# Splitting the transfers of the attention phase into pieces of 0.13 to 0.26 MB

## The chip, the core and the metric

The kernel runs on one core of a Trainium2 chip. Time is the device time of one execution in microseconds (us); the runs of the kernel before are summed up as a median of three. The engines are PE (TensorE), ACT (ScalarE), DVE (VectorE), POOL (GpSimd) and SP (SyncE), which here does nothing but issue transfers (DMAs) between the chip's memory (DRAM) and the core's own memory.

## What is computed

A chunked attention whose output is the input of a mixture of 8 experts with a dense, Sinkhorn-balanced routing. Cut to what matters:

```python
# q, k, v: (4, 8, 768, 64); mem_k, mem_v: (4, 8, 8, 64)
for c in range(24):                       # chunks of 32 queries, in each of 4 batches
    ctx = slice(max(0, 32*c - 16), min(768, 32*c + 32 + 8))
    k_full = concat(mem_k, k[:, :, ctx]); v_full = concat(mem_v, v[:, :, ctx])
    a = softmax(q[:, :, 32*c:32*c+32] @ k_full.T / 8)
    out[:, :, 32*c:32*c+32] = a @ v_full
x = out as (3072 tokens, 512)
P = exp(x @ w_gate - max);  8 times: P /= row sums; P /= column sums; P *= 3072 / 8
y = sum over e of P[:, e] * (relu(x @ w1[e]) @ w2[e])      # w1: 512x1024, w2: 1024x512
```

## The kernel before

The tokens are worked through in 24 attention blocks of 128 tokens (`n` = 0 to 23), which make 6 units of 512 tokens (`u` = 0 to 5). Attention is fp32 on PE and is woven into the products of the first expert (`e` = 0) for the early units: the products of unit 0 are plain, those of later units and experts take seven products in place of eight (operands with sums and differences, each kept as two fp16 halves). Then follow experts 1 to 7 over all 6 units.

A small scheduler (`Plan`) sets the order in which each engine gets its instructions. Every piece of work is a task with an engine, a cost, a priority (its due time) and the tasks it depends on; `Plan.run` walks through a modelled clock for each engine and takes the ready task of least priority. A transfer is a task of SP: it is charged 0.5 us of SP's clock for each DMA it issues (`cost * ISSUE`) and its `dma` figure on a modelled common DMA clock. So the number of DMAs of a task is an input of the scheduler, and the order on PE, ACT, DVE and POOL can change with it. What it decides is fixed when the program is built; on the chip each engine runs its list in order and waits by semaphores.

The transfers that matter here, all from SP:

- `load_block(n)`: q and k of a block into one of two buffers each. Before, q is one DMA of 0.26 MB, and k one (two where a batch begins). The buffer of block n is that of block n - 2, so its load waits until PE has turned that block (`tq_n`, `tk_n`: four transposes on PE of q and of k).
- `load_values(n)`: v of a block, 8 to 10 DMAs of at most 57 KB, and small copies of the memory rows inside the core (`v_pair<-v_pair`, `x_room<-x_room`). `load_extra(u)`: the few k rows past the end of each block (`kx`).
- `load(e, fp, which, ...)`: a quarter of an expert's weights, 0.52 MB, w1 as two DMAs and w2 as one. It serves the first look at a weight for its maximum (`ahead="m"`, tiles `w1fm`, `w2fm`) and the load for cutting it into operands (`w1f`, `w2f`; in `weights`, for expert 0 a second time).
- `build(u, at)` makes a unit's operands `x_u`; its `keep` stores them in DRAM as `xkeep_u`, one DMA of 1.84 MB with 14336 bytes a partition. There are six, and later experts load them back.
- For units 4 and 5 the tokens themselves (`xg_g`) are stored (`gkeep_g`) and loaded back (`xs_g`), 0.52 MB each.
- `akeep_T`: the outputs of 128 tokens, 0.26 MB, stored and later loaded again.

SP issues in one order. The framework gives SP's DMAs eight semaphores in turn, and each DMA waits for the one eight places ahead of it.

On PE the names are: `tq_n`, `tk_n`, `sp_n`, `ta_n`, `xp_n`, `xt_n` for the steps of an attention block (transposes of q and k, scores, transposes of the weights, weights times v, transposes of the result); `pp` and `yp` for the plain products of unit 0; `px`, `py`, `pz` and `yx`, `yy`, `yz` for the products of the others. Where the scheduler expects PE to have no work for more than 0.4 us, `Plan.pad` fills in products on a constant (`warm`).

Of the kernel before, what the change touches and what calls it, by code (L numbers as in the profile page):

```python
# [233 lines left out]
def tile_chunked_attn_sinkhorn_moe(  # L234
# [27 lines left out]
    nc = tc.nc  # L262
    P = 128
    B, H, S, D = q.shape
# [3 lines left out]
    CH, LC, RC = 32, 16, 8  # L268
    QB = P
# [7 lines left out]
    HP = H // 2  # L277
    KT = DM // P
# [7 lines left out]
    DH = DM // 2  # L286
    BU = UT // QB
# [46 lines left out]
    xkeep = [dram.tile([P, 2 * 7 * 2 * GT], F16, name=f"xkeep_{u}") for u in range(NU)]  # L334
    gkeep = [dram.tile([P, KT * GT], F32, name=f"gkeep_{g}") for g in range(2 * NU)]
# [3 lines left out]
    add = plan.add  # L339
# [193 lines left out]
    wo = {}  # L533
    known = {}

    def load(e, fp, which, prio, ahead="", eng="SP", after=()):
        shape = [P, 2, KT, P] if which == 1 else [P, 2, DM]
        place = "stage", stage
        if (e, which) == (0, 2) and ahead == "" and fp < 2:

            place = ("ws", "ss")[fp], comb
        st = buf(*place, shape, F32, f"w{which}f{ahead}_{e}_{fp}")

        queue = nc.scalar if eng == "ACT" else nc.sync

        def go():
            if which == 1:
                for fh in range(2):
                    queue.dma_start(st.t[:, fh], w1v[e, fp, :, :, fh])
            else:  # L550
                queue.dma_start(st.t, w2v[e, fp])

        return st, add(eng, 2 if which == 1 else 1, go, after, prio, [st], dma=2.1)

    def most(e, fp, which, st, deps, prio):
        def go():
# [160 lines left out]
        wo[0, fp, 2] = (first2[fp], [done])  # L717

    def weights(e, fp, which, prio):
        st, ld = load(e, fp, which, prio - 25)  # L720
        cut(e, fp, which, st, ld, prio)


# [36 lines left out]
    def rows(src, b, t, m):  # L760
        return src[b, :, t : t + m].rearrange("h t d -> t h d")
# [70 lines left out]
    def load_block(n):  # L832

        b, blk = divmod(n, NB)
        t0 = blk * QB
        at = needed(n) - 25.0 if n >= BU else BLOCKS[n]
        qt = buf("q", att, [P, H, D], F32, f"q_{n}")
        kt = buf("k", att, [P, H, D], F32, f"k_{n}")

        def go_k():  # L840
            if blk == 0:
                nc.sync.dma_start(kt.t[0:LC], rows(k, b, 0, LC))
                nc.sync.dma_start(kt.t[LC:P], rows(k, b, 0, P - LC))
            else:
                nc.sync.dma_start(kt.t, rows(k, b, t0 - LC, P))

        lq = add(
            "SP", 1, lambda: nc.sync.dma_start(qt.t, rows(q, b, t0, QB)), (), at, [qt], dma=1.55
        )
        lk = add("SP", 2 if blk == 0 else 1, go_k, (), at + 0.1, [kt], dma=1.55)  # L850
        state[n] = (qt, kt, lq, lk)

    vs = {}
# [258 lines left out]
    def values(n, s, made):  # L1112

        vt, lv = vs[n]
        at = needed(n) - 4.0
        aT = buf("at", att, [P, HP, QB], F32, f"at_{n}")
        tp = bank("att", [P, HP, QB], f"ta_{n}")
        xp = bank("early" if n == 1 else "two", [P, 2, 512], f"xp_{n}")
        tx = bank("att", [P, HP, QB], f"xt_{n}")
        g, o = divmod(n * QB, GT)  # L1120
        if g not in halves:
            halves[g] = (buf("g", att, [P, KT, GT], F32, f"xg_{g}"), [])
        gt = halves[g][0]

        def go_t():
            for i in range(HP):
                nc.tensor.transpose(  # L1127
                    tp.t[:, i], s.t[:, 2 * i : 2 * i + 2].rearrange("p h d -> p (h d)"), ident
                )

        def go():
            for i in range(HP):
                for c in range(CB):
                    cs = slice(c * CH, (c + 1) * CH)
                    for par in range(2):
                        r = slice(par * D, (par + 1) * D)
                        nc.tensor.matmul(  # L1137
                            xp.t[cs, par, i * DV : (i + 1) * DV],
                            aT.t[r, i, cs],
                            vt.t[r, c, i],  # L1140
                            start=True,
                            stop=True,
                        )

        t = add("PE", 0.5, go_t, [made], at, [s, aT], takes=tp)
        t = add("ACT", 0.6, lambda: nc.scalar.copy(aT.t, tp.t), [t], at, [aT], frees=tp)
        t = add("PE", 0.9, go, [t] + lv, at + 2, [vt, aT], takes=xp, many=n > 1)
        after_v.append(t)
        xq = buf("at", att, [P, HP, 2, D], F32, f"xq_{n}")
        rec = buf("sm", att, [P, H], F32, f"rec_{n}")  # L1150

        def share():
            x = xp.t[:, :, 0 : HP * DV].rearrange("p a (i d) -> p a i d", d=DV)
            r = rec.t.rearrange("p (a i) -> p a i", a=2)
            nc.vector.tensor_scalar_add(r, x[:, :, :, D], 1e-9)
            nc.vector.reciprocal(rec.t, rec.t)
            nc.vector.tensor_tensor(
                xq.t.rearrange("p i a d -> p a i d"),
                x[:, :, :, 0:D],
                r[:, :, :, None].broadcast_to([P, 2, HP, D]),  # L1160
                op=ALU.mult,
            )

        t = add("DVE", 1.1, share, [t], at + 2, [xq, rec], frees=xp)
        if n == 1:

            def hand_over(t=t):
                pstack.close()
                late["ps"] = ctx.enter_context(tc.tile_pool(name="pl", bufs=1, space=PSUM))
                del plan.free["early"]  # L1170
                for b in range(2):
                    heappush(plan.free["main"], (t.end + 0.2, b))

            add("-", 0.0, hand_over, [t], -2000.0, takes=Bank("early", lambda b: None))

        def go_x():
            for i in range(HP):
                nc.tensor.transpose(tx.t[:, i], xq.t[:, i].rearrange("p a d -> p (a d)"), ident)  # L1178

        t = add("PE", 0.5, go_x, [t], at + 2, [xq, gt], takes=tx)  # L1180
        t = add(
            "ACT",
            0.6,
            lambda: nc.scalar.copy(gt.t[:, :, o : o + QB], tx.t),
            [t],
            at + 2,
            [gt],
            frees=tx,
        )
        halves[g][1].append(t)  # L1190
        if n % (GT // QB) == GT // QB - 1 and g > 1:

            col = BU + g - 2

            def most():
                nc.vector.tensor_reduce(
                    vmax[:, col : col + 1],
                    gt.t.rearrange("p k n -> p (k n)"),
                    axis=AX.X,
                    op=ALU.max,  # L1200
                    apply_absolute_value=True,
                )

            at = needed(n) - 1.0
            vfound.append(add("DVE", 1.21, most, halves[g][1], at, [gt]))
            if g % 2:
                scale_x(n // BU, vmax[:, col - 1 : col + 1], vfound[col - 1 : col + 1], at)
        if g >= 2 * KEEP:
            if n % (GT // QB) == GT // QB - 1:
                gkept[g] = add(  # L1210
                    "SP",
                    1,
                    lambda: nc.sync.dma_start(gkeep[g], gt.t.rearrange("p k n -> p (k n)")),
                    halves[g][1],
                    needed(n) + 4.0,
                    [gt],
                    dma=2.1,
                )
        elif n % BU == BU - 1:
            build(n // BU, needed(n))  # L1220
        if n % BU == BU - 1:
            logits(n // BU, needed(n) + 6.0)
# [3 lines left out]
    def rebuild(u, at):  # L1226

        for g in (2 * u, 2 * u + 1):
            st = buf("stage", stage, [P, KT, GT], F32, f"xs_{g}")
            ld = add(  # L1230
                "SP",
                1,
                lambda st=st, g=g: nc.sync.dma_start(
                    st.t.rearrange("p k n -> p (k n)"), gkeep[g]
                ),
                [gkept[g]],
                at - 12.0,
                [st],
                dma=2.1,
            )  # L1240
            halves[g] = (st, [ld])
        build(u, at)


    def build(u, at):
# [4 lines left out]
        ready = c1 + c2 + [sxs[u]]  # L1250

        def keep(at, done):
            xkept[u] = add(
                "SP",
                1,
                lambda: nc.sync.dma_start(xkeep[u], x.t.rearrange("p a o k n -> p (a o k n)")),
                done,
                at + 10.0,
                [x],
                dma=7.0,  # L1260
            )
# [917 lines left out]
    for fp, s in enumerate(fetch_first(1, START)):  # L2179
# [9 lines left out]
        dma=0.3,  # L2189
# [3 lines left out]
    for n, (e, u) in enumerate(units):  # L2193
# [80 lines left out]
        if n >= NU and n % NU < NU - 2:  # L2274
# [16 lines left out]
                        dma=7.0,  # L2291
# [36 lines left out]
```

## Time and profile before

| what | value |
|---|---|
| median of 3 runs | 1921.87 us (1920.07 to 1922.44) |
| the profiled execution | 1919.81 us |
| its span, first to last instruction | 1917.9 us |
| granted TensorE clock | 1.000 |
| transfers | 254.82 MB in 246791 packets, 133 GB/s over the span |

The span is divided by engine and by stretch of time; a stretch of 40 or 50 us shows PE's busy time in it, the share of time for which the 16 DMA engines were busy, and the rate. The times of SP in the timeline are those of the issuing instructions: the shortest of most kinds take 0.32 to 0.39 us, and the time until the data has landed is not in them.

### The profile page before, as it was taken

The page shows a single profiled execution, that of the slowest core. Times are in us where ns is not written, and L with a number is a line of the kernel's source. Part 1 is how long each engine was busy: PE and PEld are TensorE (multiplying, and loading weights), DVE is VectorE, ACT ScalarE, POOL GpSimd, SP SyncE. Part 2 cuts the span into 40 slices and gives each one's busy share as a digit, 9 for nine tenths or more (in the row PEclk, how much of TensorE's full clock was granted, in tenths as well). Part 3 has the DMA queues.
Part 4 walks back from the last instruction along what each step waited for, and adds up shares of the span by engine and source line. Part 5 has one row for each costly group of instructions (what it writes and reads, how often), then busy time and mean ns, then how long its engine had stood idle before and what let it go on. Part 6 is the DMA issues. An engine that isn't in the chain of part 4 may idle for free.

```text
span 1917.9 us, 47295 instructions
## 1 busy us (share of the span) xinstructions
PE 1903.2 (99%) x19616; PEld 1641.0 (86%) x19616; DVE 1436.4 (75%) x2396; ACT 1033.6 (54%) x2019; POOL 524.4 (27%) x549
## 2 busy tenths in 40 slices
PE   9999999999999999999999999999999999999999
PEld 7777676688888888888888888888888888888888
DVE  6776569778679866898668875898678885786565
ACT  4765565556456545646445554655555554564453
POOL 1220001544224221432124231342124232332112
PEclk9999999999999999999999999999999999999999
DMA  8678753453235342265214533245313732322321
GB/s 198 174 194 209 171 172 116 129 204 125 83 110 172 127 148 85 78 197 185 92 63 149 197 105 127 78 160 176 138 45 105 242 122 94 100 83 84 127 83 67
DMA packets 246791, 254.82 MB, mean 133 GB/s; under 512 B 113264, under 2 KB 180272, under 8 KB 242224
## 3 DMA queue, kind: packets, MB, share of 16 engines
q1 hardware_dynamic: 244452, 251.21, 41.2%
q8 instruction: 153, 2.51, 0.6%
q10 hardware_dynamic: 2124, 0.59, 0.2%
q14 instruction: 62, 0.51, 0.1%
HBM read 187.84 MB, written 63.44 MB: 131 GB/s over the span
## 4 chain that ended last, share of the span: by engine, by line
PE 96%; DMA 2%; DVE 1%; ACT 0%; issue 0%; SPq 0%; ACTq 0%; DVEq 0%
PE px L1598 26%; PE yx L1598 23%; PE pz L1598 13%; PE yz L1598 11%; PE py L1598 6%; PE yp L2126 6%; PE yy L1598 6%; DMA q<-in_q_dram 1%; PE xp L1137 1%; PE sp L1069 1%; PE pp L2045 1%; PE tq L1006 1%; PE tk L1010 0%; PE ta L1127 0%; PE xt L1178 0%; DVE w L521 0%
## 5 line engine op out<-in xcount | busy, mean ns | idle before, releaser
L1598 PEld LDWEIGHTS <-w 128*128 128x128 f16 x7896 | 771.4, 98 | 91.9 <-issue 0.6
L1598 PEld LDWEIGHTS <-h 128*128 128x128 f16 x7056 | 690.4, 98 | 81.4 <-issue 1.5
L1598 PE MATMUL px<-x,w 128*128 128x256 f16 x4512 | 549.1, 273 | 0.0
L1931 POOL TENSOR_TENSOR acc<-acc,y 128x256 f32<-128x256 f32 x252 | 267.5, 1068 | 862.1 <-ACT y L1906 842.7
L1598 PE MATMUL yx<-w,h 128*128 128x256 f16 x4032 | 467.5, 273 | 1.3 <-DVE acc L1941 1.3
L1657 ACT ACTIVATE q<-px 128x256 f32<-128x256 f32 x376 | 142.8, 381 | 294.2 <-PE px L1598 289.5
L1598 PE MATMUL pz<-x,w 128*128 128x256 f16 x2256 | 278.2, 273 | 0.0
L1598 PE MATMUL yz<-w,h 128*128 128x256 f16 x2016 | 233.8, 273 | 0.0
L1826 DVE TENSOR_TENSOR h<-ss,h 128x1024 f16<-128x1024 f32 x160 | 215.0, 1346 | 4.0 <-ACT h L1802 3.5
L1777 ACT ACTIVATE h<-c 128x768 f16<-128x768 f32 x168 | 140.8, 838 | 106.4 <-DVE c L1667 106.4
L1802 ACT CAST h<-ss 128x1024 f16<-128x1024 f32 x168 | 174.1, 1039 | 20.4 <-DVE ss L1766 19.6
L1766 DVE SCALAR_TENSOR_TENSOR ss<-c,ss 128x256 f32<-128x256 f32 x336 | 168.3, 501 | 8.2
L1810 DVE SCALAR_TENSOR_TENSOR h<-c,h 128x768 f16<-128x768 f32 x168 | 165.3, 984 | 9.2 <-ACT h L1777 9.1
L1667 DVE SCALAR_TENSOR_TENSOR c<-px,q 128x256 f32<-128x256 f32 x188 | 78.0, 422 | 103.2 <-PE px L1598 94.9
L1906 ACT ACTIVATE y<-yx,pscale 128x256 f32<-128x256 f32 x168 | 79.4, 473 | 114.8 <-PE yx L1598 110.6
L1598 PE MATMUL py<-x,w 128*128 128x256 f16 x1128 | 139.2, 273 | 0.0
L2126 PE MATMUL yp<-w,h 128*128 128x512 f16 x576 | 132.0, 379 | 0.0
L1667 DVE SCALAR_TENSOR_TENSOR c<-py,q 128x256 f32<-128x256 f32 x188 | 78.5, 422 | 60.2 <-PE py L1598 56.7
L1766 DVE SCALAR_TENSOR_TENSOR ss<-c,h 128x512 f32<-128x512 f32 x168 | 120.8, 719 | 3.1 <-ACT h L1754 3.0
L1598 PE MATMUL yy<-w,h 128*128 128x256 f16 x1008 | 116.9, 273 | 0.0
L2126 PEld LDWEIGHTS <-h 128*128 128x128 f16 x576 | 56.0, 98 | 57.9
L513 ACT ACTIVATE w<-ws,sw 128x1024 f16<-128x1024 f32 (+1 forms) x64 | 69.3, 1089 | 65.5 <-POOL ws L602 65.5
(158 smaller groups left out, 1773.0 us busy)
## 6 DMA issues: line engine op xcount, KB each, us to landing
x<-xkeep SPq DMA_DIRECT2D x28, 1792.0 KB
akeep<-acc SPq DMA_DIRECT2D x168, 256.0 KB
acc<-akeep SPq DMA_DIRECT2D x168, 256.0 KB
w1f<-in_moe_w_dram SPq DMA_DIRECT2D x72, 256.0 KB
w2f<-in_moe_w_dram SPq DMA_DIRECT2D x32, 512.0 KB
w1fm<-in_moe_w_dram SPq DMA_DIRECT2D x56, 256.0 KB
w2fm<-in_moe_w_dram SPq DMA_DIRECT2D x28, 512.0 KB
xkeep<-x SPq DMA_DIRECT2D x6, 1792.0 KB
```

Source lines behind the costliest of these rows:

```text
L513: lambda: nc.scalar.activation(dst(0), src(), AF.Copy, scale=s),
L1598: nc.tensor.matmul(dst.t, a, b, start=(not more and n == 0), stop=(n == end), skip_group_check=more,)
L1657: lambda: nc.scalar.activation(t.t, src.t, AF.Copy, scale=DOWN),
L1667: lambda: nc.vector.scalar_tensor_tensor(c.t[:, o], src.t, DOWN, q.t, op0=ALU.mult, op1=ALU.add),
L1766: lambda: nc.vector.scalar_tensor_tensor(dst(), src(), 0.0, other(), op0=ALU.max, op1=op),
L1777: lambda: nc.scalar.activation(h.t[:, 0, 0:3], c.t, AF.Relu),
L1802: lambda: nc.scalar.copy(h.t[:, 0, 3:7], ss.t),
L1810: lambda: nc.vector.scalar_tensor_tensor(h.t[:, 1, 0:3].rearrange("p a n -> p (a n)"), c.t.rearrange("p a n -> p (a n)"), 0.0, h.t[:, 0, 0 ...
L1826: lambda: spare.tensor_tensor(h.t[:, 1, 3:7], ss.t, h.t[:, 0, 3:7], op=ALU.subtract),
L1906: (lambda: nc.scalar.activation(t.t, src.t, AF.Copy, scale=f))
L1931: lambda: nc.gpsimd.tensor_tensor(acc.t[:, cols], acc.t[:, cols], q.t, op=ALU.add),
L2126: nc.tensor.matmul(py.t, hf.t[:, hl, where[fh], o : o + P], room(fp, WIDE * wl + DM * fh, WIDE * wl + DM * (fh + 1)), start=(fp == 0 and i ...
```

## The change

The diff in full, but for some lines of context:

```diff
+    def each(to, of):
+        for i in range(KT):
+            nc.sync.dma_start(to[:, i], of[:, i])
+
-    def load(e, fp, which, prio, ahead="", eng="SP", after=()):
+    def load(e, fp, which, prio, ahead="", eng="SP", after=(), again=False):
...
+        parts = KT if (e, ahead) == (1, "m") or (e == 0 and again) else 1
+
         def go():
-            if which == 1:
+            if parts > 1:
+                for i in range(KT):
+                    j, k = i // 2, slice(i % 2 * 2, i % 2 * 2 + 2)
+                    if which == 1:
+                        queue.dma_start(st.t[:, j, k], w1v[e, fp, :, k, j])
+                    else:
+                        d = slice(i % 2 * DH, (i % 2 + 1) * DH)
+                        queue.dma_start(st.t[:, j, d], w2v[e, fp, :, j, d])
+            elif which == 1:
                 for fh in range(2):
                     queue.dma_start(st.t[:, fh], w1v[e, fp, :, :, fh])
             else:
                 queue.dma_start(st.t, w2v[e, fp])
 
-        return st, add(eng, 2 if which == 1 else 1, go, after, prio, [st], dma=2.1)
+        return st, add(eng, max(parts, 2 if which == 1 else 1), go, after, prio, [st], dma=2.1)
...
     def weights(e, fp, which, prio):
-        st, ld = load(e, fp, which, prio - 25)
+        st, ld = load(e, fp, which, prio - 25, again=True)
...
                 nc.sync.dma_start(kt.t[LC:P], rows(k, b, 0, P - LC))
+            elif n < BU:
+                nc.sync.dma_start(kt.t, rows(k, b, t0 - LC, P))
             else:
-                nc.sync.dma_start(kt.t, rows(k, b, t0 - LC, P))
+                halved(kt.t, rows(k, b, t0 - LC, P))
+
+        def halved(to, of):
+            for h in (slice(0, HP), slice(HP, H)):
+                nc.sync.dma_start(to[:, h], of[:, h])
+
+        def go_q():
+            if n < BU:
+                nc.sync.dma_start(qt.t, rows(q, b, t0, QB))
+            else:
+                halved(qt.t, rows(q, b, t0, QB))
 
         lq = add(
-            "SP", 1, lambda: nc.sync.dma_start(qt.t, rows(q, b, t0, QB)), (), at, [qt], dma=1.55
-        )
-        lk = add("SP", 2 if blk == 0 else 1, go_k, (), at + 0.1, [kt], dma=1.55)
+            "SP", 1 if n < BU else 2, go_q, (), at, [qt], dma=1.55
+        )
+        lk = add("SP", 1 if n < BU and blk else 2, go_k, (), at + 0.1, [kt], dma=1.55)
...
                 gkept[g] = add(
                     "SP",
-                    1,
-                    lambda: nc.sync.dma_start(gkeep[g], gt.t.rearrange("p k n -> p (k n)")),
+                    KT,
+                    lambda: each(gkeep[g].rearrange("p (k n) -> p k n", k=KT), gt.t),
...
             ld = add(
                 "SP",
-                1,
-                lambda st=st, g=g: nc.sync.dma_start(
-                    st.t.rearrange("p k n -> p (k n)"), gkeep[g]
-                ),
+                KT,
+                lambda st=st, g=g: each(st.t, gkeep[g].rearrange("p (k n) -> p k n", k=KT)),
...
         def keep(at, done):
+            def go():
+                to = xkeep[u].rearrange("p (a o k) -> p a o k", a=2, o=7)
+                for i in range(7):
+                    nc.sync.dma_start(to[:, :, i], x.t[:, :, i].rearrange("p a k n -> p a (k n)"))
+
             xkept[u] = add(
                 "SP",
-                1,
-                lambda: nc.sync.dma_start(xkeep[u], x.t.rearrange("p a o k n -> p (a o k n)")),
+                7,
+                go,
```

Here `KT` = 4, `BU` = 4, `H` = 8, `HP` = 4, `DH` = 256. So q and k come in halves of four heads from block 4 on (k not where a batch begins, which was two DMAs already); the second load of expert 0's w1 and the first look at expert 1's weights come in four; the stores and loads of the kept tokens in four; each `xkeep` in seven, one for each operand block, in pieces of 1024 bytes. Nothing else of the computation changes. SP issues 125 DMAs more, all between about 36 us and 320 us of the profiled execution; before and behind that the orders of all engines are the same.

In that stretch the scheduler also arranges the work anew. The first place is SP's list around the store of unit 0's operands and the loads of block 8 (`q_8`, `k_8`). Before:

```order
L549 DMA w1f_0_0_1408<-in_moe_w1_dram 128x4x128 x2
L2150 DMA akeep_0_134<-acc_0_0_1398 128x512
L549 DMA w1f_0_1_1423<-in_moe_w1_dram 128x4x128 x2
L1256 DMA xkeep_0_116<-x_0_626 128x7168
L848 DMA q_8_1463<-in_q_dram 128x8x64
L845 DMA k_8_1564<-in_k_dram 128x8x64
L790 DMA kx_2_1589<-in_k_dram 32x8x64 x3
L787 DMA kx_2_1589<-in_k_dram 16x8x64
```

and now:

```order
L2179 DMA akeep_0_134<-acc_0_0_1403 128x512
L1280 DMA xkeep_0_116<-x_0_626 256x1x512 x7
L557 DMA w1f_0_0_1516<-in_moe_w1_dram 128x2x128 x4
L557 DMA w1f_0_1_1574<-in_moe_w1_dram 128x2x128 x4
L865 DMA q_8_1604<-in_q_dram 128x4x64 x2
L865 DMA k_8_1622<-in_k_dram 128x4x64 x2
L804 DMA kx_2_1669<-in_k_dram 32x8x64 x3
L801 DMA kx_2_1669<-in_k_dram 16x8x64
```

The same bytes stand ahead of `q_8`, with the store now ahead of both weights; `q_8` was SP's 118th DMA and its halves are the 135th and 136th.

The second place follows on it, up to the load of block 9. Before:

```order
L788 DMA kx_2_1589<-in_k_dram 16x8x64
L549 DMA w1f_0_2_1670<-in_moe_w1_dram 128x4x128 x2
L890 DMA v_pair_159<-in_mem_v_dram 8x4x64 x2
L921 DMA v_pair_159<-in_v_dram 56x4x64 x8
L549 DMA w1f_0_3_1789<-in_moe_w1_dram 128x4x128 x2
L2150 DMA akeep_1_135<-acc_0_1_1461 128x512
L848 DMA q_9_1810<-in_q_dram 128x8x64
L845 DMA k_9_1846<-in_k_dram 128x8x64
L898 DMA v_pair_159<-v_pair_159 8x3x260 x2
```

and now:

```order
L802 DMA kx_2_1669<-in_k_dram 16x8x64
L557 DMA w1f_0_2_1720<-in_moe_w1_dram 128x2x128 x4
L916 DMA v_pair_159<-in_mem_v_dram 8x4x64 x2
L947 DMA v_pair_159<-in_v_dram 56x4x64 x8
L557 DMA w1f_0_3_1860<-in_moe_w1_dram 128x2x128 x4
L924 DMA v_pair_159<-v_pair_159 8x3x260 x2
L2179 DMA akeep_1_135<-acc_0_1_1461 128x512
L865 DMA q_9_1905<-in_q_dram 128x4x64 x2
```

Between the kx row of 16 that ends the first place (L787, now L801) and `q_9` stood 16 DMAs, and now 22: four more by the weights' quarters, and the two copies inside `v_pair`, which came behind block 9's q and k before.

The third place is PE's list at the same point: the four transposes of q of block 8 (`tq_8`). Rows of one product that repeat are left out. Before:

```order
L1137 MATMUL xp_6_1723<-x_room_163,at_6_1648 32x65 x32
L1006 MATMUL tq_8_1757<-ident_98,q_8_1463 128x128 x4
L2045 LDWEIGHTS w1_0_3_708
L2045 MATMUL pp_0_1_3_0_1711<-x_0_626,w1_0_3_708 128x256
...
L1010 MATMUL tk_8_1776<-ident_98,k_8_1564 128x128 x4
L1178 MATMUL xt_6_1783<-ident_98,xq_6_1765 128x128 x4
L1127 MATMUL ta_7_1792<-ident_98,s_7_1673 128x128 x4
```

and now:

```order
L1163 MATMUL xp_6_1725<-x_room_163,at_6_1658 32x65 x32
L2074 LDWEIGHTS w1_0_3_707
L2074 MATMUL pp_0_1_3_0_1708<-x_0_626,w1_0_3_707 128x256
...
L2155 LDWEIGHTS h_0_0_806
L2155 MATMUL yp_2_1771<-w2_0_0_1101,h_0_0_806 128x512
...
L1204 MATMUL xt_6_1791<-ident_98,xq_6_1768 128x128 x4
L1153 MATMUL ta_7_1797<-ident_98,s_7_1680 128x128 x4
L1032 MATMUL tq_8_1803<-ident_98,q_8_1604 128x128 x4
```

Six `pp` products, six `yp` products and eight transposes now stand between `xp_6` and `tq_8`. One more group of six `yp` products stands ahead of `tq_9` than before. In the whole program PE has 9 `warm` products more (177 against 168); the others are the same.

## Prediction

> **What bounds the kernel now.** I read the page's first lines, then the table by stretch of time, then what PE waits for.
>
> ```profile
> span 1917.9 us, 47295 instructions
> PE 1903.2 (99%) x19616; PEld 1641.0 (86%) x19616; DVE 1436.4 (75%) x2396; ACT 1033.6 (54%) x2019; POOL 524.4 (27%) x549
> ```
>
> PE is idle for 1917.9 - 1903.2 = 14.7 us in all. Its work does not change, so this is the most that a change of transfers could win, and where it lies says how much of it is in reach. The columns below are the stretch, its length, then busy time (and instructions) of PE, PEld, DVE, ACT and POOL, the clock, the DMA engines' busy share and GB/s.
>
> ```profile
> 0.00:30.00 30.00, 26.19 (x436) 21.18 (x437) 13.39 (x30) 10.71 (x22) 4.95 (x12) 1.00 0.79 180
> 30.00:60.00 30.00, 28.91 (x519) 22.98 (x517) 26.86 (x45) 23.11 (x43) 2.90 (x3) 1.00 0.81 186
> 60.00:100.00 40.00, 38.00 (x788) 28.06 (x787) 27.63 (x47) 26.85 (x54) 11.78 (x16) 1.00 0.68 186
> 100.00:150.00 50.00, 47.75 (x759) 35.62 (x758) 33.46 (x59) 30.94 (x64) 6.86 (x9) 1.00 0.78 194
> 150.00:200.00 50.00, 49.00 (x934) 36.83 (x933) 34.58 (x66) 28.43 (x61) 3.88 (x6) 1.00 0.84 208
> 200.00:250.00 50.00, 49.99 (x885) 34.65 (x884) 26.73 (x55) 29.92 (x62) 3.72 (x5) 1.00 0.67 173
> 350.00:400.00 50.00, 50.00 (x366) 35.55 (x364) 41.56 (x54) 31.45 (x58) 27.05 (x27) 1.00 0.59 194
> ```
>
> The first 30 us are before the change takes hold, and from 200 us PE has no gap to give. Between 60 and 200 us it is idle for 2.00 + 2.25 + 1.00 = 5.25 us. That is the reach of this change: 0.27% of the time, and a measurement of this kernel tells about 0.2% (3.8 us) from no change. PE's own waits for q (us in total, times, longest), and then, from its timeline, the places (the bracket holds the idle time ahead of the row).
>
> ```profile
> PE tq L1006 <- DMA q<-in_q_dram: 2.4, 3, 1.1
> ```
>
> ```profile
> 66.71 0.85 PE L1137 MATMUL xp<-x_room,at 64*32 64x65 f32 x64 [0.89 <-DVE lg L1430]
> ...
> 87.14 0.86 PE L1137 MATMUL xp<-x_room,at 64*32 64x65 f32 x64
> 89.10 0.66 PE L1006 MATMUL tq<-ident,q 128*128 128x128 f32 x4 [1.10 <-DMA q<-in_q_dram]
> ...
> 103.42 0.63 PE L1006 MATMUL tq<-ident,q 128*128 128x128 f32 x4 [0.35 <-DMA q<-in_q_dram]
> ...
> 131.80 0.35 PE L1137 MATMUL xp<-v_pair,at 64*32 64x65 f32 x16 [1.68 <-issue]
> 132.37 0.63 PE L1010 MATMUL tk<-ident,k 128*128 128x128 f32 x4 [0.22 <-PE xp L1137]
> 178.03 0.66 PE L1006 MATMUL tq<-ident,q 128*128 128x128 f32 x4 [1.00 <-DMA q<-in_q_dram]
> ```
>
> The q of blocks 8, 9 and 15 comes late, by 1.10, 0.35 and 1.00 us. The wait of 1.68 us stands inside the products with v; nothing visible releases it, and a late piece of v is my guess. The 0.89 us hang on DVE and stay. So PE runs a hair behind its loads, and what decides is when they land. The chain of waits shows how long two of these loads are under way, and the timeline of SP what it issues around them.
>
> ```profile
> 79.01 10.05 DMA q<-in_q_dram
> 98.94 4.34 DMA q<-in_q_dram
> ```
>
> ```profile
> 75.70 0.94 SPq L549 DMA_DIRECT2D w1f<-in_moe_w_dram  x2
> ...
> 78.32 0.60 SPq L1256 DMA_DIRECT2D xkeep<-x  x1
> 79.01 0.45 SPq L848 DMA_DIRECT2D q<-in_q_dram  x1
> 79.55 5.50 SPq L845 DMA_DIRECT2D k<-in_k_dram  x1
> 85.10 5.05 SPq L790 DMA_DIRECT2D kx<-in_k_dram  x3
> 90.19 0.45 SPq L787 DMA_DIRECT2D kx<-in_k_dram  x1
> ...
> 98.40 0.45 SPq L2150 DMA_DIRECT2D akeep<-acc  x1
> 98.94 0.38 SPq L848 DMA_DIRECT2D q<-in_q_dram  x1
> ...
> 100.50 1.98 SPq L898 DMA_DIRECT2D v_pair<-v_pair  x2
> ```
>
> Block 8's q lands 10.05 us after its issue because 1.84 MB of `xkeep` go ahead of it; SP itself is held for some 10 us (k 5.50 and kx 5.05 us, where q took 0.45). From 90.19 on it runs freely: 16 DMAs to 98.40, so 8.21 / 16 = 0.51 us each. That is the price of an issue here.
>
> **The change part by part.** *More issues.* Of the 125 new DMAs, those of a store or of weights cost SP time only while SP is not held up by data on its way: then 0.51 us each, else nothing. In the row of 10 us of held SP an extra issue is free; in the row of 8.21 us none is.
>
> *The load of block 8's q.* PE came to it at 87.14 + 0.86 = 88.00. Now six `pp`, six `yp` and eight transposes are ahead of it:
>
> ```profile
> 89.76 0.66 PE pp L2045 x6
> ...
> 90.85 0.44 PE xt L1178 x4
> 91.28 0.44 PE ta L1127 x4
> 91.72 1.29 PE yp L2126 x6
> ...
> 109.32 1.29 PE yp L2126 x6
> ```
>
> 0.66 + 1.29 + 0.44 + 0.44 = 2.83, so PE comes at 90.83 (the fence is the chain of waits; its last row is used below). The load: the same bytes stand ahead of it, and the stretch began with 75.70 and landed at 79.01 + 10.05 = 89.06. It now begins seven issues deeper in SP's list (the halves of q and k of blocks 4 to 7), 0 to 7 x 0.51 = 3.6 us later. SP was partly held in that time too, so I take the middle, 1.8 us: landing at 90.9, no wait to speak of, where 1.10 us was. Term -1.1 us (bounds -1.1, and with the 1.8 us of the next paragraph 94.5 - 90.83 - 1.10 = +2.5).
>
> *The size of a piece in DRAM.* `xkeep` goes out in rows of 1024 bytes in place of 14336. What that costs the DMA engines the trace doesn't show directly; the rate while they are busy is 194 / 0.59 = 329 GB/s at 350 to 400 us and 208 / 0.84 = 248 at 150 to 200, where small packets dominate. For 1.84 MB that is 5.6 or 7.4 us, so 0 to 1.8 us later for what follows a store. I take 0, since the stretch up to `q_8` (four w1f, the akeep and the q of 256 KB each, and `xkeep`) is 3.41 MB in 89.06 - 75.70 = 13.36 us, 255 GB/s, so at the lower rate already; the 1.8 stays in the range.
>
> ```profile
> w1f<-in_moe_w_dram SPq DMA_DIRECT2D x72, 256.0 KB
> ...
> xkeep<-x SPq DMA_DIRECT2D x6, 1792.0 KB
> ```
>
> *The load of block 9's q.* SP comes free 1.8 us later than at 90.19. Up to `q_9` it has six more DMAs: four of weights at 0.51, and the two copies that now come first, at 1.98 + 0.1. That is 1.8 + 2.0 + 2.1 = 5.9 us: issue at 104.8, landing after the same 4.34 us at 109.2. PE came there at 103.42 - 0.35 = 103.07; it has lost the 1.10 us wait and has one more group of `yp` (1.29) ahead, so 103.26. Wait 5.9 us where 0.35 was: term +5.6. Bounds: all hidden except the copies, 98.94 + 2.1 + 4.34 = 105.4, a wait of 2.1 (+1.8), less 0.5 if PE can begin with the first half (0.13 MB at the 248 GB/s above); with everything late and slow, 98.94 + 3.6 + 1.8 + 4.1 + 4.34 = 112.8, when PE, held 3.6 us by block 8 already, comes at 106.9: the same 5.9 on top of that.
>
> *The waits behind it.* PE is then some 4 us later against its loads, which covers 1.68 + 0.22 + 1.00 us: term -2.9 (bounds -2.9 to 0).
>
> *Warm products.* Nine more, 0.109 us each by the row below (the next row begins at 33.38: 3.50 / 32): +1.0 us (0 if they fall into a wait).
>
> ```profile
> 29.88 3.67 PE L427 MATMUL warm<-ident 128*128 128x256 bf16 x32
> ```
>
> *An added wait on SP.* `akeep_3` now stands ahead of v of block 10, `xkeep_1` and k of block 11. SP comes to it 23 issues after `q_9`, 104.8 + 23 x 0.51 = 116.5; PE has the outputs at about 115 (the last `yp` group of that tile ended at 109.32 + 1.29 = 110.6, and PE is some 4 us later), so it holds nobody, unless PE stalls a few us more, and then the loads behind it slip with it.
>
> *Kept tokens.* `gkeep` and `xs` in fours lie at 230 to 290 us, beside a PE with no gap; cost 0, and by 24 issues, 12 us, they would be late only if SP were full there.
>
> Sum: -1.1 + 5.6 - 2.9 + 1.0 = **+2.6 us** on the profiled 1919.81 (span 1917.9 and 1.9 around it). The median of the runs is 1921.87, 2.1 above it; on that, **1924.5 us**.
>
> **A rule that speaks against the change.** The Trainium skill, "DMA: Bandwidth & Descriptors", section "Rules for kernel authors", asks for 1 MiB or more in a DMA for bandwidth and to coalesce small ones. Its section "Anatomy of one DMA — SWDGE (gpsimd) path" gives a fixed cost of about 2.0 us, fitted for those issued by GpSimd; an estimate by that page for six more pieces in four stores, one after the other, would be 6 x 4 x 2.0 = 48 us. The trace speaks against paying it in sequence: 16 DMAs went out in 8.21 us, though one q took 4.34 us to land, so they overlap.
>
> **The rivals.**
>
> *SP runs out* (slower). Between the loads of block 8 and 23, SP issues 226 DMAs now and 313 then.
>
> ```profile
> 249.23 0.40 SPq L848 DMA_DIRECT2D q<-in_q_dram  x1
> ...
> 264.13 0.66 PE L1006 MATMUL tq<-ident,q 128*128 128x128 f32 x4
> ```
>
> From 79.01 to 249.23 are 170.2 us. At 0.51 us the 226 take 115, so SP is held for 55 us; 313 take 160, which leaves 10. The last load has 264.13 - 249.23 - 4.34 = 10.6 us to spare. So PE stalls once more than 20 of the 55 us stay. With half of them, 28, the stall is about 7 us: 1921.87 + 7 + 1 = 1930; with all, 34: 1957. For it: SP's rows stand end to end. Against: data that hold SP up are the same bytes, and a quarter of weights is issued in less time than it takes to move. This is also what the skill's rule would do here.
>
> *The pieces slip into held time* (faster). Then q of block 8 and 9 and the later waits are all on time: -1.10 - 0.35 - 2.9 + 1.0 = -3.4, 1918.5 us. For it: no load waits behind a whole store. Against: the engines still move the 1.84 MB first, and `q_9` has the copies ahead of it.
>
> *It does nothing that counts*: new waits as large as the old ones, and the warm products: +1.0, 1922.9 us.
>
> **How the numbers follow.** Forecast 0.46, SP runs out 0.30, slipped in 0.14, nothing that counts 0.10. Faster by over 0.2% (below 1918.0) needs nearly the whole 5.25 us: 0.05, out of the third case. Slower (above 1925.7): the 0.30 and a third of the forecast's 0.46, whose bounds reach -2.7 to +9.1 us: 0.45. The rest, 0.50, is the same. The range, 1918.5 to 1936, leaves out the end of the second case above half its price and little below.
>
> **What would show it.** PE's wait at `tq` of block 8 gone and one of 4 to 7 us at `tq` of block 9 with q as its releaser, issued near 104.8; no other wait above 1 us up to 200 us; SP's `xkeep` pieces taking longer than 0.4 us each, held by data. If `tq` of blocks 14 to 23 waits for q or k as well, SP ran out. If PE has no wait for q at all, the issues were hidden. The prediction falls if the q of block 9 lands by 104, or if a gap opens behind 200 us.

## The result and the profile after

| | before | after |
|---|---|---|
| median of 6 runs each | 1921.06 us (1919.13 to 1922.44) | 1932.46 us (1929.91 to 1935.09) |
| ratio, 95% interval | | 1.0061 (1.0051 to 1.0072) |
| the profiled execution | 1919.81 us | 1933.22 us |
| its span | 1917.9 us | 1931.3 us |
| granted TensorE clock | 1.000 | 0.998 |

The change costs 11.4 us. That lies inside the predicted range, but it is not the case that was held likeliest: it is the first rival, in which SP runs out of time to issue.

The first lines of the page, the kernel after:

```profile
span 1931.3 us, 47477 instructions
PE 1909.0 (99%) x19625; PEld 1642.7 (85%) x19625; DVE 1435.0 (74%) x2396; ACT 1035.3 (54%) x2019; POOL 522.9 (27%) x549
```

Of the span's 13.4 us more, PE's idle time has 22.3 - 14.7 = 7.6 us and its busy time 1909.0 - 1903.2 = 5.8 us. The busy time is not nine warm products alone (1.0 us): the clock stood at half of full speed in two stretches of 3.41 us (shown below), and that is 3.4 us of products that took longer. Of the other 1.4 us a part is a late second half of q, which shows as a longer `tq` (0.89 and 0.94 us for blocks 8 and 9, against 0.66 and 0.63 before); the rest is open. The stretches of time, in the columns of the prediction:

```profile
30.00:60.00 30.00, 28.89 (x517) 23.02 (x518) 26.22 (x44) 22.95 (x43) 2.07 (x2) 1.00 0.74 181
60.00:100.00 40.00, 36.99 (x694) 26.82 (x692) 24.62 (x40) 25.38 (x50) 8.12 (x11) 1.00 0.66 173
100.00:150.00 50.00, 46.98 (x836) 35.29 (x834) 32.44 (x63) 30.81 (x63) 10.44 (x15) 0.97 0.75 191
150.00:200.00 50.00, 46.81 (x790) 32.67 (x792) 30.28 (x55) 27.50 (x59) 3.53 (x5) 1.00 0.67 177
200.00:250.00 50.00, 47.64 (x827) 32.07 (x821) 28.03 (x59) 25.72 (x53) 4.17 (x6) 0.97 0.64 169
```

Between 60 and 200 us PE is now idle for 3.01 + 3.02 + 3.19 = 9.22 us (5.25 before), and from 200 to 250 us, where it had no gap, for 2.36 us. Over these stretches the DMA engines are no busier: 0.67 in place of 0.84 from 150 to 200 us. So on the whole it isn't the data that have no room, though in bursts they fill the engines (0.98 from 197 to 200 us). Where the gaps stand (PE's timeline, after):

```profile
93.00 0.89 PE L1032 MATMUL tq<-ident,q 128*128 128x128 f32 x4 [1.25 <-DMA q<-in_q_dram]
96.81 0.63 PE L820 MATMUL tx<-ident,kx 128*128 128x128 f32 x4 [0.83 <-DMA kx<-in_k_dram]
...
109.22 0.94 PE L1032 MATMUL tq<-ident,q 128*128 128x128 f32 x4 [2.73 <-DMA q<-in_q_dram]
110.00 4.44 PE L2155 MATMUL yp<-w,h 128*128 128x512 f16 x12
...
197.48 0.63 PE L1204 MATMUL xt<-ident,xq 128*128 128x128 f32 x4 [2.51 <-DVE xq L1183]
...
208.41 0.27 PE L494 MATMUL row_x<-ident,most_of 128*1 128x128 f32 x1 [2.36 <-DVE most_of L445]
```

The three gaps of 2.4 to 2.7 us make 7.6 us together. Of these only the first names a load. The other two name DVE, but DVE itself waited (its timeline, and then SP's, around them):

```profile
195.08 1.22 DVE L572 TENSOR_REDUCE mxs<-w2fm 128x1 f32<-128x1024 f32 x1 [4.69 <-DMA v_pair<-in_v_dram]
...
196.65 0.69 DVE L1183 TENSOR_TENSOR xq<-xp,rec 128x512 f32<-128x512 f32 x1
...
204.01 1.22 DVE L572 TENSOR_REDUCE mxs<-w2fm 128x1 f32<-128x1024 f32 x1 [2.24 <-DMA w2fm<-in_moe_w_dram]
205.52 1.22 DVE L572 TENSOR_REDUCE mxs<-w2fm 128x1 f32<-128x1024 f32 x1 [0.30 <-DMA v_pair<-in_v_dram]
206.66 1.21 DVE L1222 TENSOR_REDUCE vmax<-xg 128x1 f32<-128x1024 f32 x1
```

```profile
188.64 1.93 SPq L560 DMA_DIRECT2D w2fm<-in_moe_w_dram  x4
...
196.30 1.04 SPq L865 DMA_DIRECT2D q<-in_q_dram  x2
197.44 1.00 SPq L865 DMA_DIRECT2D k<-in_k_dram  x2
198.54 4.46 SPq L560 DMA_DIRECT2D w2fm<-in_moe_w_dram  x8
203.10 4.71 SPq L947 DMA_DIRECT2D v_pair<-in_v_dram  x7
```

DVE works through its list in order. The maximum of a quarter of w2 (`mxs`), which nobody needs soon, stands in that list ahead of attention's `xq` and of the `most_of` that PE's `row_x` reads, and it waits for a `w2fm` that SP issues late: the eight pieces of two quarters take SP 4.46 us. For the wait that ended at 195.08 the profile names a `v_pair`, which `mxs` does not read. Later `v_pair` DMAs use the same semaphores as the four pieces issued from 188.64 on, so the name is the profile's guess; by the trace's semaphore records the last part of the fourth piece came at 194.89. Its other fifteen parts had come by 192.58, so half of that wait is one slow part of a transfer and not the issue. For the gap at 208.41 the chain of waits shows the way from the last of the eight pieces to DVE:

```profile
201.42 0.43 SPq L560
201.85 0.04 issue
201.89 3.51 DMA w2fm<-in_moe_w_dram
205.40 0.03 issue
205.43 0.05 DVEq L572
205.48 0.04 issue
205.52 1.22 DVE mxs L572
```

A late load that PE never touches reaches PE through an engine in between.

The clock, in stretches of 3.41 us around the three gaps (same columns; the clock is the third number from the right):

```profile
107.12:110.53 3.41, 1.21 (x7) 0.76 (x8) 2.72 (x6) 1.82 (x3) 0.00 (x0) 1.00 0.90 199
110.53:113.94 3.41, 3.41 (x10) 1.22 (x9) 0.00 (x0) 0.00 (x0) 0.00 (x0) 0.50 0.49 95
...
195.86:199.27 3.41, 1.79 (x17) 1.75 (x18) 3.34 (x6) 1.08 (x2) 0.00 (x0) 1.00 0.85 221
...
206.10:209.52 3.42, 1.11 (x11) 1.04 (x12) 3.38 (x7) 0.27 (x1) 0.00 (x0) 1.00 0.30 65
209.52:212.93 3.41, 3.41 (x18) 2.36 (x16) 1.70 (x10) 1.79 (x4) 0.38 (x1) 0.50 0.84 187
```

Behind the gap of 2.73 us the clock is at half from 110.53 to 113.94: the twelve `yp` at 110.00 take 4.44 us. Behind the gap of 2.36 us it is at half from 209.52 to 212.93. Each costs 1.7 us. Behind the gap of 2.51 us, at 197.48, it stays at full speed.

### The profile page after: what moved, and what is told of

It is laid out like the page before. It is cut to its first block, busy times and chain, and to the rows that moved or that the text cites. A ratio compares the mean times of both kernels' runs of the same rounds, so it can differ in the third digit from the quotient of the medians.

```text
span 1931.3 us, 47477 instructions
## 1 busy us (share of the span) xinstructions
PE 1909.0 (99%) x19625; PEld 1642.7 (85%) x19625; DVE 1435.0 (74%) x2396; ACT 1035.3 (54%) x2019; POOL 522.9 (27%) x549
## 2 busy tenths in 40 slices
DMA packets 262873, 254.85 MB, mean 132 GB/s; under 512 B 115264, under 2 KB 199168, under 8 KB 259072
## 4 chain that ended last, share of the span: by engine, by line
PE 94%; DVE 2%; DMA 2%; SPq 1%; ACT 0%; issue 0%; ACTq 0%; DVEq 0%
PE px L1627 25%; PE yx L1627 23%; PE pz L1627 13%; PE yz L1627 11%; PE py L1627 6%; PE yy L1627 6%; PE yp L2155 6%; PE xp L1163 1%; SPq L947 1%; PE pp L2074 1%; DMA q<-in_q_dram 1%; PE sp L1095 1%; PE ta L1153 1%; PE xt L1204 0%; PE tk L1036 0%; PE tq L1032 0%
```

## The experiments

The theory: SP's time for issuing is what ran out. The rivals: the new order that the scheduler made; the pieces as data (short rows, more packets); one part of the change alone; the rule that a DMA waits for the one eight places ahead, which more DMAs also meet more often. A ratio is to the kernel before on the same chip, with its 95% interval.

**The pieces in the old order.** The scheduler is charged as before, so that PE, DVE, ACT and POOL keep the order of before, but SP issues all the pieces.

```diff
-add(eng, max(parts, 2 if which == 1 else 1), go, ...)
+add(eng, 2 if which == 1 else 1, go, ...)
...
-lq = add("SP", 1 if n < BU else 2, go_q, ...)
+lq = add("SP", 1, go_q, ...)
```

(and so for k, `gkeep`, `xs` and `xkeep`.)

> The pieces of the change, but each task charged to the scheduler as before, so that PE, DVE, ACT and POOL have the order of before and SP issues the pieces in place of the whole transfers. Theory A (SP's issue time: 125 issues more at about 0.5 us make the loads late): slower than before by 5 us or more, 1926 to 1945 us, with PE waiting for q, k or v. Theory B (the new arrangement does it, above all the first looks at expert 1's w2, which now stand in DVE's order ahead of attention's steps): within 3 us of before, 1918 to 1924 us.

Measured: 1939.32 us, 1.0094 (1.0072 to 1.0115), clock 0.995.

**The new order with whole transfers.** The scheduler is charged as in the change, and each transfer goes out whole.

```diff
-for h in (slice(0, HP), slice(HP, H)):
-    nc.sync.dma_start(to[:, h], of[:, h])
+nc.sync.dma_start(to, of)
```

(and so for the weights, the kept tokens and `xkeep`.)

> The order of the changed kernel on every engine (tasks charged as with the pieces), but each transfer whole as before. Theory A: the 125 issues are gone, so SP is ahead again; 1920 to 1925 us, no wait of DVE for w2fm above 1 us. Theory B: the order is what costs; near the changed kernel, 1929 to 1935 us, with DVE's waits for w2fm and PE's two gaps behind them still there.

Measured: 1919.52 us, 0.9994 (0.9985 to 1.0003), clock 1.000. So the order costs nothing, and the pieces cost all of it; with the old order they cost no less. PE's waits of these two kernels (us in total, times, longest), the pieces first:

```profile
PE tq L1032 <- DMA q<-in_q_dram: 6.9, 3, 3.3
PE tk L1036 <- DMA k<-in_k_dram: 4.3, 1, 4.3
```

```profile
PE tq L1030 <- DMA q<-in_q_dram: 1.0, 2, 0.7
```

In the old order PE waits for q and k directly; in the changed kernel half of the waiting was carried through DVE. With the same new order and whole transfers, DVE's list is the same and its `mxs` waits hardly at all; the longest of the three waits that were 4.69, 2.24 and 0.30 us is this one:

```profile
195.65 1.22 DVE L571 TENSOR_REDUCE mxs<-w2fm 128x1 f32<-128x1024 f32 x1 [0.84 <-DMA w2fm<-in_moe_w_dram]
```

So the order alone does not make these loads late. Whether the charged order also wins something back, 1932.46 against 1939.32, is likely but barely separated: the two intervals meet at 1.0072.

**Issues without pieces.** The kernel before with its order and its whole transfers, and behind each of the transfers that the change splits, as many more DMAs as it would add, of 512 bytes each (128 rows of 4 bytes) into a tile that nobody reads: 125 in all.

```diff
+nc.sync.dma_start(spare_in[:, i : i + 1], w_gate[0:P, 0:1])
```

> The kernel before, in its own order and with whole transfers, but behind each transfer that the change splits SP issues as many more DMAs as the split adds, 125 in all, each a column of 128 numbers (512 bytes) into a scrap tile that nothing reads. It parts the issue of a DMA from the data it moves. If the loss is SP's time for issuing (theory A): as slow as the pieces in the old order (1939), 1930 to 1945 us. If it is in the pieces themselves (rows of 1024 bytes, more packets for the DMA engines): within 4 us of before, 1918 to 1924 us.

Measured: 1946.69 us, 1.0130 (1.0115 to 1.0145). The summary of that one line of code (shortest, median and longest in ns, first and last start in us), then PE's waits:

```profile
L543 SPq DMA_DIRECT2D spare_in<-in_moe_w_gate_dram x125: 327/503/2230, 38.2 to 351.6; - x125
```

```profile
PE tq L1022 <- DMA q<-in_q_dram: 8.2, 4, 4.4
PE xt L1194 <- DVE xq L1173: 6.9, 3, 5.7
PE tk L1026 <- DMA k<-in_k_dram: 5.4, 1, 5.4
```

125 nearly empty DMAs hurt at least as much as the pieces (the intervals meet at 1.0115), and by waits of the same kinds: q, k, and DVE's `xq`. Each holds SP for a median of 0.503 us, against 0.48 to 0.62 us for the pieces of q, k and `xkeep` in the changed kernel. So neither the bytes nor the length of the rows is needed for the loss. The number of packets is not parted off by this run: the page counts 264792 of them here and 262873 in the changed kernel, against 246791 before. The runs below part it off. A further rival, the rule of eight places, does not fit SP's list: between the loads of block 8 and block 23 SP of the changed kernel stands between two DMAs for over 0.15 us only 6 times, 2.5 us in all (18 times and 17.1 us before). It has more DMAs and fewer waits; the time goes into the issuing instructions themselves.

**One part undone at a time.** The scheduler is charged to match each.

```diff
-parts = KT if (e, ahead) == (1, "m") or (e == 0 and again) else 1
+parts = KT if e == 0 and again else 1
```

> The change without the split of the first look at expert 1's weights (w1fm, w2fm as before: 12 DMAs in place of 32 for that; the scheduler is charged for what is issued). If the two PE gaps behind w2fm (2.51 and 2.36 us, and the low clock after the second) come from these loads being late, they go: 1924 to 1927 us. If lateness is general (SP full), the gaps come up at other loads: 1929 to 1934 us.

```diff
-for i in range(7):
-    nc.sync.dma_start(to[:, :, i], x.t[:, :, i]...)
+nc.sync.dma_start(xkeep[u], x.t...)
```

> The change without the split of the stores of the operands (xkeep in one DMA as before, 36 issues fewer). Theory A with issue time counting everywhere: 36 x 0.5 to 0.7 us of SP are free again, so a third of the loss or more goes: 1924 to 1929 us. If SP is held by the data of a store anyway, so that its pieces cost nothing: 1930 to 1935 us.

```diff
-halved(qt.t, rows(q, b, t0, QB))
+nc.sync.dma_start(qt.t, rows(q, b, t0, QB))
```

(and so for k.)

> The change without the halves of q and k (37 issues fewer, the scheduler charged accordingly). Theory A with equal price for every issue: 37 of 125, so some 4 us back: 1926 to 1930 us. If the halves are what helps (PE starts on the first half of q earlier): slower than the change, above 1934 us.

```diff
-for i in range(KT):
-    nc.sync.dma_start(to[:, i], of[:, i])
+nc.sync.dma_start(to, of)
```

> The change without the split of the kept tokens (gkeep, xs; 24 issues fewer, all behind 240 us). PE has only 0.7 us of gaps there in the changed kernel, so I expect nothing: 1930 to 1934 us. If SP's list has to be worked off at the pace of its issues up to the last block, 24 x 0.5 = 12 us of SP time come back at the end and up to 3 us of it show: 1928 to 1930 us.

| whole again | us | ratio, interval | longest waits of PE |
|---|---|---|---|
| first look at w1, w2 of expert 1 | 1930.14 | 1.0044 (1.0027 to 1.0061) | DVE `xq` 3.9, q 3.8 |
| `xkeep` | 1928.85 | 1.0042 (1.0027 to 1.0057) | q 4.0, ACT `c` 3.1 |
| q and k | 1926.55 | 1.0027 (1.0016 to 1.0039) | q 4.5 |
| `gkeep`, `xs` | 1932.04 | 1.0055 (1.0040 to 1.0070) | DVE `most_of` 3.5 |

None brings the time of before back, and in each a wait comes up at another place. So no one part holds the loss. Only q and k are told from the whole change by their interval. That parts issues from packets: with q and k whole there are 37 DMAs fewer but only 593 packets fewer than in the changed kernel (262280), while whole `xkeep` takes away 36 DMAs and 10561 packets (252312) and wins no more. It is the count of DMAs that SP pays for. The pieces of the kept tokens, which are issued behind 240 us, cost nothing that can be told.

**Fewer issues than before.** If SP were the bound of the kernel before too, fewer issues would be faster. There, w1's quarters in one DMA of 0.52 MB, 64 issues fewer in the program, but only 12 of them up to 150 us:

```diff
-for fh in range(2):
-    queue.dma_start(st.t[:, fh], w1v[e, fp, :, :, fh])
+queue.dma_start(st.t, w1v[e, fp].rearrange("p kt fh f -> p fh kt f"))
...
-return st, add(eng, 2 if which == 1 else 1, ...)
+return st, add(eng, 1, ...)
```

> The opposite of the change: the kernel before with every quarter of w1 in one DMA of 0.52 MB in place of two (64 issues fewer in the program, 12 of them up to 150 us, the scheduler charged accordingly). Theory A: SP has a little more room in attention; 1916 to 1920 us, at most the 5 us that PE is idle between 60 and 200 us. If larger transfers hold up q and k: 1922 us or more.

Measured: 1920.47 us, 1.0000 (0.9991 to 1.0009). So little more room for SP buys the kernel before nothing that can be told; a larger saving in the attention phase was not tried without other changes.

**Stores issued by ACT.** Four kernels tried to take issues off SP. The changed one with `akeep` of the first expert and the pieces of `xkeep` on ACT's queue:

```diff
-nc.sync.dma_start(to[:, :, i], ...)
+nc.scalar.dma_start(to[:, :, i], ...)
...
-"SP", 1, lambda: nc.sync.dma_start(akeep[T], a.t), ...
+"ACT", 1, lambda: nc.scalar.dma_start(akeep[T], a.t), ...
```

> The changed kernel with all its pieces, but the stores of unit 0's outputs and of the operands (akeep of expert 0, 24 DMAs, and the 42 pieces of xkeep) are issued by ACT in place of SP, the scheduler charged accordingly. The data and their sizes are the same. Theory A (SP's time): 66 issues off SP are half of the 125 added, so half of the loss or more goes: 1921 to 1927 us. If the pieces themselves cost, or ACT becomes late by its 66 issues (about 30 us in 250): 1930 us or more.

Measured: 1949.33 us, 1.0151 (1.0136 to 1.0167). The kernel before with only the 24 `akeep` on ACT (the last two lines above):

> The kernel before with the 24 akeep stores of expert 0 issued by ACT, which makes those outputs, in place of SP. Theory A: SP has 24 issues less, and no longer waits for ACT there; of PE's 5 us of gaps between 60 and 200 us some go: 1916 to 1919.5 us. If SP's room no longer matters at this level: 1920 to 1922 us.

Measured: 1939.31 us, 1.0100 (1.0084 to 1.0116). And the kernel before with `akeep` and whole `xkeep` on ACT and w1 in one:

> The kernel before with akeep of expert 0 and xkeep issued by ACT and every quarter of w1 in one DMA: 42 issues fewer on SP up to 320 us. Theory A at its other end: PE's gaps between 60 and 200 us shrink from 5 us to 2 or less: 1915.5 to 1918.5 us. If ACT's added issues make its own work late: 1921 us or more.

Measured: 1946.17 us, 1.0135 (1.0119 to 1.0152). All three were expected to be faster and are slower. In these, two things had changed together, since a task that moves to ACT also changes the order. The last kernel holds the order: the changed kernel, its scheduler charged as it is, with the same 66 stores issued by ACT at their place in the program.

> The changed kernel with all its orders on PE, DVE, ACT and POOL kept, but the 24 stores akeep of the first expert and the 42 pieces of xkeep issued by ACT at the place in the program where SP issued them; SP loses 66 issues. If the loss is SP's time for issuing, and the three slow kernels with stores on ACT were slow through their new orders alone, this one is faster than the changed kernel: some 50 of the 66 issues stand ahead of block 23's q, and at 0.15 to 0.2 us each, as measured, they give 7 to 10 us back: 1921 to 1926 us, gaps of PE at tq under 2 us. If a store issued by ACT costs something itself (ACT is held by it, so that rows for PE come late), it is 1935 us or more, with PE waiting for ACT. If the two cancel, 1928 to 1935.

Measured: 1957.28 us, 1.0195 (1.0179 to 1.0212): slower still, as in the rival of that expectation. ACT's timeline there:

```profile
116.75 6.85 ACTq L1280 DMA_DIRECT2D xkeep<-x  x6
123.64 0.27 ACT L1049 COPY kC<-kxT 128x96 f32<-128x96 f32 x1 [6.81 <-DMA xkeep<-x]
```

Six pieces hold ACT for 6.85 us, and its own work stands still behind them; PE then waits 3.65 us for ACT's `s`, in front of `ta` at 125.04. The issue time was not saved but moved to an engine whose list PE waits for. The Trainium skill, "DMA: Bandwidth & Descriptors", section "Issuing engines are not separate DMA queues", says that to issue from several engines only saves the time of the sequencer that starts the DMA, "which is usually small relative to the DMA itself". Here it was the scarce thing.

But the two longest waits of PE there, 7.23 and 4.87 us, are for q, which SP issues with 66 DMAs fewer in its list. SP came late because it was held by ACT's stores. PE's row, and what SP waited for (us in total, times, longest):

```profile
248.23 1.20 PE L1032 MATMUL tq<-ident,q 128*128 128x128 f32 x4 [7.23 <-DMA q<-in_q_dram]
```

```profile
SPq L916 <- DMA xkeep<-x: 14.0, 1, 14.0
```

The eight semaphores go in turn to the DMAs of both queues, in the order of the program: in the trace each of the eight belongs to DMAs of SP and of ACT. So a DMA of SP can wait for a store eight places ahead that ACT has not yet issued. From 231.16 to 245.22 SP stood still like that; ACT issued the store's pieces from 238.96 on.

The second miss shows the same. There `akeep` costs ACT only 24 x 0.326 us, but SP waits for it again and again:

```profile
SPq L921 <- DMA akeep<-acc: 19.9, 6, 6.6
```

DVE's and PE's timelines of that kernel:

```profile
181.31 1.22 DVE L558 TENSOR_REDUCE mxs<-w2fm 128x1 f32<-128x1024 f32 x1 [11.56 <-DMA w2fm<-in_moe_w_dram]
182.45 0.68 DVE L1083 TENSOR_REDUCE sm<-sp 128x8 f32<-128x512 f32 x1
```

```profile
184.57 1.11 PE L1127 MATMUL ta<-ident,s 128*128 128x128 f32 x4 [8.13 <-ACT s L1108]
```

It is the trap of the changed kernel again, larger: `mxs` stands ahead of attention's `sm` in DVE's list, and its `w2fm` was issued only at 177.66, after SP had waited from 163.52 to 170.13 for stores that ACT issued at 167.72. What the new order adds to this was not tried by itself. So these four kernels do not show what relief of SP alone would bring; that remains open.

No kernel tried beats the one before.

## Why the prediction was wrong in its likeliest case, and right in a rival

**The price of an issue: right.** From 95.16 to 105.98 us SP of the changed kernel runs freely:

```profile
95.16 1.97 SPq L557 DMA_DIRECT2D w1f<-in_moe_w_dram  x4
97.17 0.71 SPq L916 DMA_DIRECT2D v_pair<-in_mem_v_dram  x2
97.92 3.92 SPq L947 DMA_DIRECT2D v_pair<-in_v_dram  x8
101.89 1.93 SPq L557 DMA_DIRECT2D w1f<-in_moe_w_dram  x4
103.87 1.54 SPq L924 DMA_DIRECT2D v_pair<-v_pair  x2
105.51 0.37 SPq L2179 DMA_DIRECT2D akeep<-acc  x1
105.98 0.99 SPq L865 DMA_DIRECT2D q<-in_q_dram  x2
```

21 DMAs in 10.82 us are 0.52 us each; 0.51 was forecast.

**Block 9's q: right in place, cause and landing, wrong in size.** Issued at 105.98 (forecast 104.8), landed at 109.68 (109.2). But PE came to it at 109.22 - 2.73 = 106.49 us and not at 103.26, since it had lost time on the way. So the term was 2.73 us, not 5.9.

**Block 8's q: wrong.** Its wait of 1.10 us was to go; it is 1.25. The stretch ahead of it began 3.07 us later (78.77 for 75.70), where 1.8 was taken. Its two halves held SP for 2.77 us at 88.73, and it landed near 93, not at 90.9; 94.5 was the bound.

**"The waits behind it are covered, -2.9": the step that failed.** It took PE's lateness as cover for later loads. The three waits that it named did go: from 118 to 197 us PE has one wait for a load, 0.62 us. But every load stands in SP's one list, and the later ones slip with it, so other waits opened: idle time between 150 and 200 us rose from 1.00 to 3.19 us. The step looked only at loads that PE reads. The larger losses, 2.51 and 2.36 us, came through DVE, from a `w2fm` that the prediction costed at its issue alone.

**SP runs out: what happened.** SP's row for the load of block 23:

```profile
270.32 0.94 SPq L865 DMA_DIRECT2D q<-in_q_dram  x2
```

From 88.73 to 270.32 are 181.6 us for 313 issues, 0.58 us each; before it was 170.2 us for 226. Of the 55 us of held time 181.6 - 160 = 22 us are left, just past the 20 from which the rival said that PE stalls. By its budget that is a stall of only some 1 to 2 us, where PE's idle time grew by 7.6. The budget looked at the last load alone, which was on time in the end (PE has no wait there), while loads in between were late first. It also let the stretch begin at 79.01; it began 9.7 us later. The rival's 1930 us is 2.5 below the measured time; it had reckoned 7 us of stall from 28 us of kept time, and had no term for the clock. So its mechanism was right, and that its number came so near is in part luck. Its weight, 0.30, was too small: "a quarter of weights is issued in less time than it takes to move" spoke against it, but the eight pieces of `w2fm`, 1.05 MB, took SP 4.46 us, 0.56 us each, no less than free-running issues do. Since the DMA engines were nearly full just then (0.98 and 0.87 from 197 to 203 us), this one place doesn't tell issue from data; the experiments do.

**The test named the wrong loads.** "`tq` of blocks 14 to 23 waits for q or k" was to show that SP ran out. There is only one such wait over 0.5 us (0.62 at 167.92). The other sign, a gap behind 200 us, is there.

**The clock: missing.** No term stood for it. It is 3.4 of the 13.4 us of the span, and more in the pieces with the old order (17.1 us at half clock, so 8.5 us).

**Right as costed:** the kept tokens at 0 (undone, 1932.04 against 1932.46 us), and the short rows in DRAM: nothing in the runs asks for a price, as empty DMAs beside whole stores lose no less than the pieces do. The nine warm products do show as 1.0 us of PE's busy time in the new order with whole transfers (1904.2 against 1903.2 us), but that kernel is not slower, so as a term of the time they are not shown. Nothing tried the added wait of `akeep_3` by itself.

## What to carry to other kernels

An engine that only issues transfers has a budget too: count its DMAs between two deadlines, multiply by the free-running time of one (0.5 us here), and see how much is left; splitting a transfer spends that budget, and moving it to a compute engine spends that engine's, and can hold the first engine too where both share semaphores. Follow a late load through every engine that reads it: an in-order list puts urgent work behind a wait that nobody hurries for. And give a gap of about 2 us or more on PE a second price, for the clock behind it: 1.7 us each here.

## What the hardware showed that was not expected

- The clock fell to half for 3.41 us behind gaps of 2.73 and 2.36 us, and not behind one of 2.51 us at 197.48. The Trainium skill, "TensorE: Matmul & The Clock Gate", section "HAM oscillation — how this bites in real kernels", puts the bound at gaps over about 3.4 us; these were shorter. That page's section "Part 1: The HAM clock gate (the "warmup" mystery)" calls the window of that length free-running. The trace agrees: the clock changes at 110.53, 113.94, 209.52 and 212.93, and from 113.94 to 209.52 are 28 times 3.41 us. On that grid the two gaps that cost put 2.20 and 2.31 us of idle time into one stretch, while the gap of 2.51 us lies across an edge and puts at most 1.62 us into one. In the traces of all fourteen kernels here, a stretch at full clock with up to 1.70 us of idle time is followed by full clock, and one with 1.90 us or more by half; between 1.81 and 1.89 us both occur.
- A DMA of 512 bytes holds SP about as long as one of 0.13 to 0.26 MB: a median of 0.503 us, against 0.48 to 0.62.
- ACT pays about the same for a piece of `xkeep` as SP does, a median of 0.596 against 0.620 us, and its compute instructions wait meanwhile.
